# Sinkhorn of batch 0 in a chain of its own, the output projection of two batches by Strassen blocks, and an order of work given as a table

## The chip, the cores and the metric

The kernel runs on one core of a Trainium2 chip. The core has five engines that run side by side, each with its own queue of instructions that it takes in order: TensorE (PE, matrix products, into the eight PSUM banks), VectorE (DVE), ScalarE (ACT), GpSimd (POOL), and SyncE (SP), which here issues DMA transfers. TensorE loads the stationary operand of a matmul by a separate instruction (PEld). The metric is device time in microseconds (us), as a median over runs. Lower is better.

## The reference

Inputs q, k, v are of 4 batches, 8 heads, 768 positions, 64 features; `sort_net` gives an 8 by 8 matrix for each batch and head; the three weights of the second part are 512 by 1536, 512 by 1536 and 1536 by 512.

```
P = sort_net
for _ in range(5):
    P = exp(P - max(P, last axis))
    P = P / (sum(P, last axis) + 1e-9)        # rows
    P = P / (sum(P, second last axis) + 1e-9) # columns
k_sorted = einsum('bhij,bhjcd->bhicd', P, k_b)   # 8 blocks of 96 positions are mixed
v_sorted = the same with v
scores = q_b @ k_sorted_b.T / 8                  # within a block: 96 by 96
attn = softmax(scores);  x = attn @ v_sorted_b   # to 3072 tokens of 512
out = ((x @ w_a) * (x @ w_b)) @ w_out
```

## The kernel before

**A planner.** The kernel describes its work as pieces (`add`): an engine or a choice of engines with a duration for each, what a piece waits for, which buffers it gets and puts back, and a rank. `Plan.solve` walks through time greedily: of the pieces that could start first on each engine it takes the one of the lowest rank, at the engine that would end it first, and advances that engine's clock by the planned duration. The start times give the order in which the instructions are issued, so every engine's queue is in that order, and the planned durations (`LAT`, `EPS`, `AT` and the numbers at each `add`) matter only through it. `_fill` puts matmuls on a dummy tile (`warm_sb`) into the planned gaps of TensorE up to 32.6 us.

**Loads.** q, k, v and the weights come by DMAs that GpSimd issues and that turn fp32 into bf16 on the way, at most seven in flight (`load`). Batch 0 comes first, pair of heads by pair of heads, then column blocks 0 to 3 of `w_a` and `w_b` (`load_ab`, 384 columns each), the second halves of q of batch 0 in between, then batch 1, `w_out`, batch 2. GpSimd issues them in its one queue together with its elementwise work.

**Sinkhorn.** All 32 matrices lie in one tile `p_nat`, a partition for each batch and head (lines 412 to 425). A turn is an exp on ScalarE and six operations on VectorE: row sum, reciprocal, multiply, column sum, reciprocal, multiply. After five turns the result is widened (`p_rep`, half by VectorE, half by ScalarE) and brought across the partitions by eight small matmuls (`spread_ops`, line 435); `spread` (line 440) multiplies it with a mask into `s_all`, the matrix by which TensorE mixes blocks of k and v. The part of batch 0 is read from PSUM by VectorE; the others are spread later by GpSimd from a copy `p_col`.

**Attention.** For each pair of heads: transpose q, mix k and v by `s_all`, bring v to the layout that is needed, scores, exp, product with v, division by the row sum, and x transposed (`xT`). Batch 0 is done in halves of four blocks, so that the projections can start early; later batches send v, x, and in batch 3 also q, through DMA (V through DRAM, x and q by transposing DMAs), issued by SP.

**Projections.** Batch 0 uses plain products (`ab_plain`, line 749: for 12 column blocks and 2 halves of the tokens, four matmuls of 384 columns with `w_a`, four with `w_b`, then the gated product hT). Batches 1 to 3 use a Strassen scheme with seven products for eight (`ab_strassen`, line 831), which needs sums of weight blocks (`w_sums`, 16 operations, GpSimd alone) and of x blocks (`x_sums`), snapshots of PSUM by ScalarE (line 840) and additions by VectorE. All elementwise sums go through the helper `tt`, line 306.

**Output.** `out_plain` (line 899) does, for each batch, 2 halves of tokens by 3 chunks: twelve matmuls of 512 columns, a copy out of PSUM by ScalarE or VectorE (`copy`, lines 248 and 250), and two stores issued by SP (line 919). hT has one buffer, so gated products of the next batch wait for the output matmuls that read it (`out_last`).

The softmax here doesn't subtract the row's maximum and nothing guards it: scores larger than these inputs give would overflow.

## Time and profile before

| what | value |
|---|---|
| median of 3 runs | 245.04 us (244.59 to 245.09) |
| profiled execution | 245.06 us, of which the span of the core is 243.3 us |
| granted TensorE clock | 1.000 |
| busy: PE, DVE, ACT, POOL | 233.7, 150.1, 125.3, 119.6 us |
| matmuls | 2204 |
| DMA | 27.90 MB; the 16 engines are busy without a break from about 6 to 60 us |

In the lines below, a group reads: source line, engine, operation, tile written <- tiles read, shape, count. In a timeline the first two numbers are start and busy time; a bracket at the end gives the engine's idle time before and what released it. In a window row the pairs are busy time and instruction count of PE, PEld, DVE, ACT, POOL, then the granted clock, the DMA share and GB/s. A busy TensorE contains the dummy matmuls of `warm_sb`. Ends of matmuls are modelled.

### The profile page before, as it was taken

Reading aid. Unit: us, or ns where it says so; the run is one execution under the profiler, and the core shown is the slowest. Engines: PE = TensorE matmul, PEld = TensorE weight load, DVE = VectorE, ACT = ScalarE, POOL = GpSimd, SP = SyncE. Lnnn points to the kernel's source line nnn. Section 1 sums busy time; section 2 is a strip of 40 time slices with the busy share of each in tenths; the row PEclk is TensorE's granted clock in tenths of the full one; section 3 lists DMA queues with packets and bytes.
Section 4 is the critical chain, followed back from the end, with each engine's and each line's share of the span. In section 5 each row is a group of like instructions: output and inputs, shape, how many; then the busy total and the mean of one; then the engine's idle time right before and its main releaser. Section 6 shows DMA issues by size and latency. Waiting matters only on the chain.

```text
span 243.3 us, 5723 instructions
## 1 busy us (share of the span) xinstructions
PE 233.7 (96%) x2204; PEld 132.4 (54%) x2204; DVE 150.1 (62%) x348; ACT 125.3 (52%) x243; POOL 119.6 (49%) x132
## 2 busy tenths in 40 slices
PE   6998999999989999999999999999999999999992
PEld 2466766666655554665544455665654455565440
DVE  6656654654555738589987452988862448886210
ACT  3366646468655533667654443766631076673100
POOL 8979999999970020069755110173540007355000
PEclk9999999999999999999999999999999999999999
DMA  5999999999965683619998867200035450000135
GB/s 67 180 203 187 202 203 187 167 191 178 162 134 107 167 184 78 149 16 154 135 175 110 192 174 178 46 0 0 3 66 108 96 122 0 1 0 3 43 86 129
DMA packets 50106, 27.90 MB, mean 115 GB/s; under 512 B 28832, under 2 KB 47008, under 8 KB 50080
## 3 DMA queue, kind: packets, MB, share of 16 engines
q0 software_dynamic: 24112, 14.16, 43.3%
q1 hardware_dynamic: 25968, 13.38, 25.7%
q8 instruction: 17, 0.28, 0.5%
q14 instruction: 9, 0.07, 0.1%
HBM read 30.29 MB, written 8.26 MB: 158 GB/s over the span
## 4 chain that ended last, share of the span: by engine, by line
PE 67%; ACT 1%; DVE 1%; issue 0%; ACTq 0%; DVEq 0%
PE ps L831 33%; PE ps L899 26%; PE ps L593 2%; PE ps L578 2%; PE ps L489 1%; PE ps L537 1%; PE ps L473 1%; PE ps L749 1%; ACT f L840 0%; DVE xp L604 0%; ACT o L248 0%; DVE a L306 0%; DVE rec L599 0%; ACTq L840 0%; DVEq L306 0%
## 5 line engine op out<-in xcount | busy, mean ns | idle before, releaser
L306 POOL TENSOR_TENSOR hT<-a,f 128x384 bf16<-128x384 bf16 x39 | 35.5, 918 | 78.1 <-DVE f L306 56.3
L899 PE MATMUL ps<-w_out_sb,hT 128*128 128x512 bf16 x288 | 66.4, 379 | 0.0
L840 ACT COPY f<-ps 128x384 f32<-128x384 f32 x108 | 48.2, 482 | 23.6 <-PE ps L831 21.1
L899 PEld LDWEIGHTS <-hT 128*128 128x128 bf16 x288 | 27.0, 98 | 30.1
L306 DVE TENSOR_TENSOR a<-f,ps 128x384 bf16<-128x384 f32 x54 | 29.4, 549 | 10.4 <-PE ps L831 6.4
L306 DVE TENSOR_TENSOR f<-f,ps 128x384 f32<-128x384 f32 x54 | 28.9, 550 | 8.9 <-PE ps L831 6.0
L583 ACT ACTIVATE eT<-ps 96x768 bf16<-96x768 f32 x32 | 24.9, 806 | 17.2 <-PE ps L578 16.9
L306 DVE TENSOR_TENSOR hT<-a,ps 128x384 bf16<-128x384 bf16 x42 | 23.1, 551 | 12.4 <-PE ps L749 6.9
L248 ACT COPY o<-ps 128x512 f32<-128x512 f32 x15 | 8.8, 585 | 36.3 <-PE ps L899 36.3
L831 PE MATMUL ps<-tx,ws_a 128*128 128x384 bf16 x108 | 25.2, 326 | 0.2 <-ACT f L840 0.2
L831 PE MATMUL ps<-tx,ws_b 128*128 128x384 bf16 x108 | 24.9, 326 | 0.3 <-ACT f L840 0.3
L604 DVE TENSOR_TENSOR xp<-ps,rec 96x512 bf16<-96x512 f32 x32 | 21.4, 677 | 0.4
L749 PE MATMUL ps<-xT,w_a_sb 128*128 128x384 bf16 x96 | 19.6, 327 | 0.0
L749 PE MATMUL ps<-xT,w_b_sb 128*128 128x384 bf16 x96 | 19.6, 326 | 0.0
L831 PEld LDWEIGHTS <-ws_b 128*128 128x128 bf16 x144 | 13.8, 98 | 10.1 <-ACT f L840 0.9
L755 ACT CAST a<-ps 128x384 bf16<-128x384 f32 x24 | 11.5, 479 | 14.9 <-PE ps L749 9.1
L250 DVE COPY o<-ps 128x512 f32<-128x512 f32 x9 | 6.2, 691 | 20.8 <-PE ps L899 20.7
L831 PEld LDWEIGHTS <-ws_a 128*128 128x128 bf16 x144 | 13.5, 98 | 10.1 <-ACT f L840 1.4
L831 PE MATMUL ps<-xT,w_b_sb 128*128 128x384 bf16 x72 | 17.6, 326 | 0.3 <-DVE xp L604 0.2
L831 PE MATMUL ps<-xT,w_a_sb 128*128 128x384 bf16 x72 | 17.5, 326 | 0.0
L831 PEld LDWEIGHTS <-w_b_sb 128*128 128x128 bf16 x108 | 10.4, 98 | 7.9 <-DVE xp L604 0.7
L831 PEld LDWEIGHTS <-w_a_sb 128*128 128x128 bf16 x108 | 10.3, 98 | 7.9 <-ACT f L840 0.6
(90 smaller groups left out, 337.9 us busy)
## 6 DMA issues: line engine op xcount, KB each, us to landing
out_dram<-o SPq DMA_DIRECT2D x48, 128.0 KB, 2.4
k<-in_k_dram POOLq DMA_DIRECT2D x16, 192.0 KB, 6.1
v<-in_v_dram POOLq DMA_DIRECT2D x16, 192.0 KB, 6.1
vd<-vm SPq DMA_DIRECT2D x10, 192.0 KB, 2.9
vs<-vd SPq DMA_DIRECT2D x10, 192.0 KB, 3.1
q<-in_q_dram POOLq DMA_DIRECT2D x16, 96.0 KB, 6.9
w_a_sb<-in_moe_w_a_dram POOLq DMA_DIRECT2D x4, 384.0 KB, 7.1
w_b_sb<-in_moe_w_b_dram POOLq DMA_DIRECT2D x4, 384.0 KB, 9.0
```

What stands on the lines that cost most here:

```text
L248: nc.scalar.copy(out=out, in_=in_)
L250: eng.tensor_copy(out=out, in_=in_)
L306: ENG[eng].tensor_tensor(out=out, in0=in0, in1=in1, op=op)
L578: nc.tensor.matmul(sc[:, e, i * BLK:(i + 1) * BLK], lhsT=kT[e * D:(e + 1) * D, at:at + P], rhs=rhs, start=True, stop=True)
L583: nc.scalar.activation(out=buf(("eT", b, p, h))[:, :, 0:HB], in_=buf(("sc", b, p, h))[0:BLK, :, 0:HB], func=AF.Exp, scale=float(scale))
L593: nc.tensor.matmul(ops_[:, e, i * OW:(i + 1) * OW], lhsT=eT[:, e, i * BLK:i * BLK + P], rhs=vs[:, h * NBH + i, e * OW:(e + 1) * OW], start ...
L604: nc.vector.tensor_tensor(out=_ap(xp, h * NBH * 2 * D, [[NB * 2 * D, BLK], [D, 2], [2 * D, NBH], [1, D]]), in0=_ap(ops_, 2, [[1024, BLK], ...
L749: nc.tensor.matmul(pf[:, 0:HW], lhsT=w_sb[:, kc, m * P:(m + 1) * P], rhs=buf(("xT", b))[:, kc, t * HW:(t + 1) * HW], start=(kc == 0), stop ...
L755: ea = add("ACT", 0.48, lambda: nc.scalar.copy(out=buf(("a", b, t, m)), in_=buf(("pf", b, t, m, "a"))[:, 0:HW]), [pa], get=[("a", ("a", b, ...
L831: nc.tensor.matmul(buf(key)[:, 0:HW], lhsT=lf(j), rhs=rf(j), start=start and j == 0, stop=j == 1, skip_group_check=not start)
L840: return add("ACT", 0.48, lambda: nc.scalar.copy(out=buf((name, b, g, n)), in_=buf(kA)[:, 0:HW]), [dep], get=[("f", (name, b, g, n))], rank=r)
L899: nc.tensor.matmul(po, lhsT=hT[:, t * 2 + m // G, m % G, c * P:(c + 1) * P], rhs=w_out_sb[:, m, :], start=(m == 0), stop=(m == KO - 1), sk ...
```

## The change

**Sinkhorn.** The eight matrices of batch 0 get a chain of their own, with a partition for each head and row (64 partitions of 8 values, `pa`). In the first turn the row sum comes with the exp (`accum_out`), and a small fp32 matmul (`sk_turn`) turns the matrices so that the other sum lies along the free axis; in the four turns that follow the row sums over partitions are a small fp32 matmul with a mask of heads (`sk_rows`), and the remaining scale goes into the next exp as its `scale`. One matmul spreads the result (`spread_first`). Four small mask operations of VectorE are added. The 24 matrices of batches 1 to 3 keep the old chain, which now starts after batch 0's and has rank 12 instead of -9; its widening is one VectorE operation into a buffer of the ring `o`.

**Output.** Batches 2 and 3 use seven products for eight on blocks of hT and `w_out`: three chunks of seven products, each six matmuls of 256 columns. It needs eight sums of `w_out` blocks (`o_sums`), 24 sums of hT blocks for each batch, nine snapshots by ScalarE and twelve additions by VectorE for each batch. The stores of the last chunk are issued half by SP and half by ScalarE.

**Order.** A table `ORDER` of 1513 entries gives which piece comes next and on which of its engines; `solve` then only works out the planned times. The model changes as well: SP's DMAs get a clock of their own (`DH`), a `port` keeps planned GpSimd and VectorE sums apart, some durations and the load rate differ. `w_sums` may use VectorE for one of the two column blocks; the weight blocks are loaded in the order 0, 2, 1, 3; the ring `o` has four buffers instead of three; the first products of a Strassen batch wait for the `p5` of the last output chunk of the batch before (`lasty`) where that has one. `warm_sb` is now a part of `ws_b`.

```diff
-            pick = None
-            for e, c in cands.items():
-                lo = min(s for s, _ in c) + self.EPS[e]
-                s, op = min(((s, o) for s, o in c if s <= lo), key=lambda x: (x[1].rank, x[1].seq))
...
+        def given():
+
+            op = self.ops[order[done] // 2]
+            assert op in ready, "ORDER is not one of these pieces of work"
+            e = list(op.alts)[order[done] % 2]
+            return begin(op, e, max(self._when(op), op.ready)), e, op
...
+            s, e, op = given() if order else greedy()
...
-STRASSEN_OUT = ()
+RATE = 365e3
+ORDER = (
+    b"&,13###+#'#7#)#A#/#3#9#C#-#%$>#5#1#=$@$B#;$D#E#?$F$H#I$J#G$L#M$N#K$P#Q$R$T%l#O#U$V%n$X#Y$Z"
...
+STRASSEN_OUT = (2, 3)
...
-    for c in range(1, 4):
+    for c in (2, 1, 3):
         load_ab(c)
...
+    def sk_turn():
+        nc.tensor.matmul(buf(bank)[0:HN, 0:NB], lhsT=p_exp.rearrange("p h j -> p (h j)"),
+                         rhs=m_row, start=True, stop=True)
+
+    def sk_rows():
+        nc.tensor.matmul(buf(bank)[0:HN, NB:2 * NB], lhsT=m_same.rearrange("p h j -> p (h j)"),
+                         rhs=pa[:, 1, :], start=True, stop=True)
...
+    x = step("PE", 0.2, sk_turn, [x, o_row], get=[("bank", bank)])
+    x = step("DVE", 0.16, lambda: nc.vector.reduce_sum(
+        out=ps1, in_=buf(bank)[0:HN, 0:NB], axis=AX.X), [x])
+    x = step("DVE", 0.15, lambda: nc.vector.reciprocal(out=pc1, in_=ps1), [x], lat=0.1)
+    for it in range(4):
+        x = step("ACT", 0.3, lambda it=it: nc.scalar.activation(
+            out=pa[:, 1, :], in_=px if it else buf(bank)[0:HN, 0:NB], func=AF.Exp, scale=pc1), [x], lat=0.2)
+        x = step("PE", 0.12, sk_rows, [x, o_same])
+        x = step("DVE", 0.2, lambda: nc.vector.reciprocal(out=pr, in_=buf(bank)[0:HN, NB:2 * NB]),
+                 [x], put=[bank], lat=0.1)
+        x = step("DVE", 0.2, lambda: stt(px, pa[:, 1, :], 1.0, pr, ps1), [x], lat=0.02)
+        x = step("DVE", 0.15, lambda: nc.vector.reciprocal(out=pc1, in_=ps1), [x], lat=0.1)
...
         last = add("ACT", 0.26, lambda: nc.scalar.activation(out=p_nat, in_=p_nat, func=AF.Exp),
-                   [last], rank=-9)
+                   [last, o_p0], rank=12)
...
-            p1 = pe(kA, lambda j, w=w: w(0, 0, j), lambda j: xb(0, 0, j), True, False, x + wd, r,
+            p1 = pe(kA, lambda j, w=w: w(0, 0, j), lambda j: xb(0, 0, j), True, False,
+                    x + wd + [st.get(("lasty", b - 1))], r,
...
+            todo = ((0, lambda g=g: (hb(1, 0, g), hb(1, 1, g)), ALU.add, h21 + h22, None),
+                    (1, lambda g=g: (sb(0, g), hb(0, 0, g)), ALU.subtract, h11, 0),
+                    (2, lambda g=g: (hb(0, 0, g), hb(1, 0, g)), ALU.subtract, h11 + h21, None),
+                    (3, lambda g=g: (hb(0, 1, g), sb(1, g)), ALU.subtract, h12, 1))
...
+            p6 = pe(kA, s(1), wt(1), False, True, [s1] + sd(1) + td(1), rk, put=sput(1) + tput(1))
+            u2 = snap("ou2", p6)
+            p5 = pe(kY, s(0), wt(0), True, True, sd(0) + td(0), rk + 0.1, get=[("bank", kY)],
+                    put=sput(0) + tput(0))
+            st["lasty", b] = p5
+            p7 = pe(kA, s(2), wt(2), False, True, [u2] + sd(2) + td(2), rk, put=sput(2) + tput(2))
+            u3 = snap("ou3", p7)
+            p4 = pe(kZ, h(1, 1), wt(3), True, True, [p1, p2] + hd(1, 1) + td(3), rk + 0.6,
+                    get=[("bank", kZ)], put=tput(3))
+            c22 = plus("ou3", kY, 1, 1, [u3, p5], [("ou3", b, c)])
+            c21 = plus("ou3", kZ, 1, 0, [u3, p4], [kZ, ("ou3", b, c), ("och", b, c)])
+            p3 = pe(kY, s(3), wo(1, 1), False, True, [c22] + sd(3), rk, put=sput(3))
+            c12 = plus("ou2", kY, 0, 1, [u2, p3], [kY, ("ou2", b, c), ("och", b, c)])
...
+                    (nc.scalar if last and u else nc.sync).dma_start(
```

## The prediction

> **What bounds the kernel now.** I read the page first, for the engines' shares and the chain of work that ended last; then the waits of TensorE; then the timeline, at the start, around the two last output stages and at the end; then the windows, to see what the other engines have free there.
>
> The page:
>
> ```profile
> span 243.3 us, 5723 instructions
> PE 233.7 (96%) x2204; PEld 132.4 (54%) x2204; DVE 150.1 (62%) x348; ACT 125.3 (52%) x243; POOL 119.6 (49%) x132
> ...
> PE 67%; ACT 1%; DVE 1%; issue 0%; ACTq 0%; DVEq 0%
> ```
>
> TensorE is busy in 96% of the span, and the chain, which begins only at 72 us, is TensorE but for 1% each of ScalarE and VectorE. "Busy" needs a second look, because the kernel also issues matmuls on a dummy tile, `warm_sb`. The timeline of the start:
>
> ```profile
> 2.29 0.26 ACT L414 ACTIVATE p_nat<-p_nat 32x64 f32<-32x64 f32 x1 [0.27 <-DMA p_nat<-in_sort_net_dram]
> ...
> 4.05 0.26 ACT L414 ACTIVATE p_nat<-p_nat 32x64 f32<-32x64 f32 x1 [1.50 <-DVE p_nat L424]
> ...
> 10.84 0.21 DVE L424 TENSOR_TENSOR p_fin<-p_nat,csum 32x64 bf16<-32x64 f32 x1
> 11.99 0.61 ACT L248 COPY p_rep<-p_fin 32x512 bf16<-32x512 bf16 x1
> 13.47 0.36 PE L435 MATMUL ps<-ident,p_rep 32*128 32x32 bf16 x8
> 13.95 1.29 DVE L440 TENSOR_TENSOR s_all<-mask,ps 128x256 bf16<-128x256 bf16 x2 [2.45 <-PE ps L435]
> 14.42 0.38 PE L500 MATMUL ps<-s_all,k 128*64 128x64 bf16 x12
> 27.46 0.82 PE L749 MATMUL ps<-xT,w_a_sb 128*128 128x384 bf16 x4
> ```
>
> Until 14.42 TensorE does four groups of q transposes (0.38 each) and otherwise dummies: the Sinkhorn chain (turns of 1.76 us, 2.29 to 4.05) is the path. From 27.46 the long projections run, four matmuls in 0.65, and TensorE is full to the last matmul at 238.68. Between them it does about 10.8 us of batch 0's attention in 13.0. After 27.46 the gaps that the timeline and chain show are 0.8 at 71.2, 0.6 at 118.4, 0.6 at 126.0, 1.2 at 151.0 and 1.1 at 210.8: 4.2 us together. So time comes off the end in three ways: an earlier end of the Sinkhorn, less TensorE work, a shorter tail.
>
> Windows around the output stages of batches 2 and 3 (busy of PE, PEld, DVE, ACT, POOL in each), and three groups behind the elementwise helper:
>
> ```profile
> 160.00:180.00 20.00, 20.00 (x125) 11.96 (x123) 16.79 (x34) 13.16 (x31) 10.58 (x12) 1.00 0.11 21
> 180.00:200.00 20.00, 20.00 (x102) 9.74 (x101) 7.33 (x14) 5.66 (x13) 1.18 (x2) 1.00 0.46 99
> ```
>
> ```profile
> L306 POOL TENSOR_TENSOR hT<-a,f x39: 910/918/925, 104.3 to 223.4; 128x384 bf16<-128x384 bf16 x39
> L306 DVE TENSOR_TENSOR tx<-xT x5: 547/550/554, 81.1 to 188.9; 128x768 bf16<-128x768 bf16 x5
> L306 POOL TENSOR_TENSOR tx<-xT,tx x1: 1831/1831/1831, 139.1 to 139.1; 128x768 bf16<-128x768 bf16 x1
> ```
>
> While a batch's gated product runs, VectorE is 84% busy; while the output projection runs it is 37% busy and GpSimd nearly idle.
>
> **The change, part by part.** The profiled execution took 245.06, 1.76 beyond its span of 243.3, and stands 0.02 above the median of 245.04; the sum is made against it.
>
> *Sinkhorn of batch 0.* A turn was exp 0.26, six VectorE operations of 0.19 to 0.25, and gaps of 0.03 to 0.04. The new turn is exp, a tiny fp32 matmul, reciprocal 0.19, multiply 0.21, reciprocal 0.19, four hand-offs of 0.03 to 0.04: 0.99 plus the matmul x. No row shows a lone fp32 matmul. Below, x is an eighth of the 0.36 group at 13.47 plus its hand-off of 0.12 to VectorE: 0.17; above, the whole group, 0.48. I take 0.40, nearer to the upper, since fp32 is unlikely to cost what bf16 does. First turn 1.63, four turns of 1.39, final multiply, matmul and hand-offs 0.50: 7.7 from 2.29, so the spread starts at 10.0. With every x low it is 8.8; with every x high and 0.2 in each turn for the accumulated sums, which no row shows, 11.6. VectorE also gets four small mask operations at the start, and the ScalarE and TensorE queues between the turns hold q copies and dummies, so I take 10.6: 3.4 earlier than 13.95 (ends 2.3 and 5.2). The p_rep copy of ScalarE and its wait (11.05 to 13.47) leave with it.
>
> Is anything late next? The last v of batch 0 is issued at 8.93 and lands 6.6 later, at 15.5, and was read at 20.92; the first weights of w_b land at 20.3 (10.89 plus 9.4) and were read at 28.12. These have 5 and 8 us to spare. But the weight loads now come in the order 0, 2, 1, 3: block 1 lands where block 2 did, w_b at 30.6, and its first reader at 32.58 moves to about 29. What hides this is the other work there (3.4 us of batch 0's second halves, and block 2's projections); without it, it costs 1.4.
>
> The Sinkhorn of batches 1 to 3, 35 operations, now comes after: on VectorE 5 times 1.26 plus a widening and a copy, about 7.5 us, on ScalarE 1.3. From 12 to 45 VectorE is idle for 13 us, and GpSimd's spreads (2.0 each), which wait for it and have the load issues behind them in their queue, are not needed before batch 1's mix at 48.37. Spread evenly it costs nothing; falling wholly before 27 it would delay the evacuations there by up to half, 3.7. I take 0.7. Front: 3.4 less 0.7, a gain of 2.7 (ends 0.5 and 4.0).
>
> *Output of batches 2 and 3 by Strassen blocks.* Out: 72 matmuls of 512 columns a batch at 0.2158 (2.59 for twelve), 15.5 us. In: three chunks of seven products of six matmuls of 256 columns, 126. That width is not in the trace. The 384 wide take 0.1626 (0.65 for four), the 128 wide transposes 0.056 with a weight load each (0.45 for eight), so weight loads are no floor, and the line between them gives 0.109: 13.7 us. Gain 1.8 a batch, 3.6 (ends 2.9 at twice the 128 wide pitch, 3.9 at half the 512's).
>
> The cover: per batch 24 sums of hT blocks; the order table gives 11 of batch 3's to GpSimd (0.92, the hT row), 13 to VectorE (two bf16 inputs; 0.35 from 0.55 for twice the width): 10.1 and 4.6 us. Nine snapshots by ScalarE (0.37, from 0.48 at 384) and twelve additions by VectorE (0.41) replace six copies of 0.59 to 0.69. Eight w_out sums come once. In 160 to 180 VectorE has 3.2 free, so some of its sums fall after the gated product, whose last hT write ends 3.7 us after the first output matmul (182.80 plus 0.56, against 179.69). TensorE has p1, p2 and p4 of three chunks, nine groups of 0.65, 5.9 us, which need no sums. That just covers 3.7, two chained sums and a short queue. In batch 2 the new dependence `lasty` holds every gated product of batch 3 behind the last chunk's p5; TensorE is in order, so a wait there stops everything. I take 0.4 a batch, 0.8 (ends 0 and 3 a batch).
>
> A row on the shared port: GpSimd's tx sum at 139.1 took 1.83 against 1.63 at 89.6; VectorE was in a sum of two bf16 tiles for its first 0.34. So GpSimd stands still for about 0.6 of such an overlap, while its hT products, beside VectorE operations with a PSUM input, keep to 910 to 925 ns. Thirteen sums of 0.35 take at most 2.7 us from it a batch, on 10 us in a stage where it has 9.4 free: inside the bound of 3. The Trainium skill (GPSIMD Engine Reference, Specifications) says that GpSimd and VectorE share SBUF interfaces and contend when VectorE reads two SBUF inputs. It speaks against this change: read as a full stop over all 13 VectorE sums, an estimate from it is 4.6 a batch where the row gives 2.7; were all of either turned into waits of TensorE in place of my 0.4, the time would be 246.3 by the page and 242.5 by the row.
>
> *Tail.* The last copy (0.59), two store issues on one queue to 240.42 and 2.87 to the end make 4.61 after 238.68. Now an addition of 0.41 and one issue of 0.57 on each of SP and ScalarE: 3.9. Gain 0.7. In the table p7 of the last chunk is followed by a sixth of p2, p5, p4, then p3: 1.41 of work against 1.33 for the addition that p3 waits for. No stall.
>
> *The order.* Of the 4.2 us of gaps a new order may close some and open others; I take a gain of 1.0 (ends a gain of 2.5, a loss of 2.0).
>
> Sum: 2.7 + 3.6 + 0.7 + 1.0 - 0.8 = 7.2; 245.06 - 7.2 = 237.9.
>
> **Rivals.** *The front hardly gains.* The later Sinkhorn and batch 0's evacuations share VectorE and ScalarE (11.9 and 12.0 of 18 us busy in 12 to 30); front 0.5, order nothing, waits 1.6: 0.5 + 3.6 + 0.7 - 1.6 = 3.2, 241.9. For it: both engines are as loaded as TensorE there. Against: the operations are small, and have until 45.
>
> *All of it comes.* Front 4.0, output 3.9, tail 0.7, order 2.5, no waits: 11.1, 234.0. For it: 5 us of slack on the last load. Against: the order must be right to tenths in five queues.
>
> *Slower: the sums come late.* In the stage before the output VectorE (21.07 of 25.2 busy from 154.5 to 179.7) has no room for 4.6 more, and GpSimd needs 12.16 + 10.1 + 2.7 of 25.2. If the last sums are later than the cover by d, TensorE stops for d in each batch. Without my 0.8 the gain is 8.0, so it decides from d = 4.0; at 6 the time is 249. Against: after 180 both engines are nearly free, and 24 sums on two engines are some 5 us even if none was done early.
>
> *No effect*: the parts cancel within 0.2% (0.5 us), about what a measurement of this kernel can tell from no change; no mechanism of its own.
>
> **How the numbers follow.** The sum, 236 to 240.2: 0.55. All of it, 233 to 236: 0.15. The front hardly gains, 240.2 to 244: 0.18. No effect 0.02, slower 0.10. Faster 0.55 + 0.15 + 0.18 = 0.88. The range 234.2 to 242.6 leaves out 0.05 below and 0.15 above.
>
> **What would show it.** Right: the first mix matmul near 11 instead of 14.4; the first long projection near 24.5; the two output stages at 0.65 for six matmuls; the last matmul near 232 with under 4 us behind it. Wrong: dummies or idle time before the output products that read the sums; VectorE or ScalarE without a gap from 11 to 27; a lone fp32 turn of 1.8 or more; matmuls of batch 0 at half their rate, as the first eleven dummies now are (0.42 for 512 columns, later 0.22), because TensorE pauses in every turn.

## The result, and the profile after

The changed kernel took 261.09 us (median; 260.23 to 262.45) against 245.03 us for the kernel before: a ratio of 1.0665, interval 1.0617 to 1.0713. It is 16 us slower where 7 us of gain were forecast. The profiled execution took 260.97 with a span of 259.2.

The page of the changed kernel, the lines that answer to those shown of before:

```profile
span 259.2 us, 6049 instructions
...
PE 236.4 (91%) x2306; PEld 144.5 (56%) x2306; DVE 178.2 (69%) x418; ACT 127.6 (49%) x257; POOL 150.0 (58%) x164
...
PEclk9999799999999999599999999999999599999999
...
PE 79%; DVE 8%; DMA 6%; issue 2%; POOL 2%; ACT 0%; DVEq 0%; ACTq 0%
```

TensorE is busy 2.7 us longer, though it has less to do, and stands 22.8 us in place of 9.6. VectorE has 28 us more and GpSimd 30 us more; both now stand in the chain, with DMA. The clock row has three notches that were not there before, in slices 5, 17 and 32 of 6.5 us each.

The waits of TensorE (engine, tile and line, what it waited for; total, times, longest):

```profile
PE ps L1145 <- DVE v L391: 5.9, 1, 5.9
PE ps L742 <- DMA vs<-vd: 4.7, 2, 4.3
PE ps L649 <- issue: 2.9, 2, 1.7
PE ps L899 <- ACT a L905: 1.3, 1, 1.3
```

Where the time went can be read from the start and end of the stages, all from the timelines of TensorE and VectorE (the last column is a version of experiment 3):

| us | before | after | later by | all three edits undone (3) |
|---|---|---|---|---|
| first spread of s_all | 13.95 | 12.28 | -1.7 | - |
| first long projection | 27.5 | 28.4 | +0.9 | 27.8 |
| output of batch 0, first matmul | 75.9 | 79.7 | +3.8 | 79.3 |
| output of batch 1, first matmul | 129.4 | 140.3 | +10.9 | 133.2 |
| output of batch 2, last matmul | 195.9 | 213.0 | +17.1 | 200.1 |
| last matmul ends | 238.7 | 254.2 | +15.5 | 241.3 |
| end of the span | 243.3 | 259.2 | +15.9 | 245.7 |

So there are three places of loss: 3.8 before the output of batch 0, 7 in that stage, 6 before the end of batch 2's output. Only behind the last one does the changed kernel gain: from the last output matmul of batch 2 to the last matmul of all it needs 41.2 us where the kernel before needs 42.8.

**The third place.** The timeline where batch 2's sums of hT blocks are made; the tiles `k` and `v` hold the sums, `tx` the x sums of batch 3:

```profile
194.75 1.10 DVE L391 TENSOR_TENSOR k<-hT 128x384 bf16<-128x384 bf16 x1
...
197.74 0.35 DVE L391 TENSOR_TENSOR v<-v,hT 128x384 bf16<-128x384 bf16 x1
198.81 3.45 POOL L391 TENSOR_TENSOR tx<-xT 128x768 bf16<-128x768 bf16 x2
...
200.69 1.78 DVE L391 TENSOR_TENSOR v<-hT 128x384 bf16<-128x384 bf16 x1
202.53 0.82 PE L1145 MATMUL ps<-q,k 128*128 128x256 bf16 x3 [5.88 <-DVE v L391]
...
206.99 0.50 PE L1145 MATMUL ps<-q,v 128*128 128x256 bf16 x3
```

A VectorE sum of this shape takes 0.35 when GpSimd rests (197.74), 1.06 to 1.10 beside GpSimd's sums of the same shape, and 1.78, twice, beside the twice as wide ones (198.81: two of them). TensorE stands 5.88 for them. Then three matmuls of 256 columns take 0.82 (0.64 from start to start) until about 206.3, where they later take 0.50 (0.33): the clock is down, which costs another 1.9.

**The second place.** The chain of work in order of time:

```profile
96.18 10.80 DMA vs<-vd
...
107.62 4.09 PE ps L1052 x10
```

TensorE waits for batch 2's V, which comes back from DRAM 10.8 us after its issue. The ten output matmuls behind it take 0.41 each in place of 0.22. The median trip of these transfers is 5.1 us here and 3.1 before. Nothing in this stage is a part of the change as I had read it; GpSimd issues the first ten of batch 3's loads at 92.2 to 100.3 here (the rest from 125 on), where the kernel before issues them all at 107.2 to 119.5, behind the last of these transfers.

In the windows of 100 to 120 and 200 to 220 us the granted clock is 0.83, in the others from 30 us to 240 it is 1.00: these are two of the notches. The third lies in the first place.

**The first place.** VectorE among GpSimd's weight sums, and TensorE in the middle of batch 0's mixing:

```profile
25.09 0.25 PE L649 MATMUL ps<-s_all,k 128*64 128x64 bf16 x4 [1.73 <-issue]
41.20 1.65 POOL L391 TENSOR_TENSOR ws_b<-w_b_sb 128x768 bf16<-128x768 bf16 x1
41.96 2.56 DVE L567 TENSOR_TENSOR p_nat<-p_nat,csum 24x64 f32<-24x64 f32 x1
...
50.94 2.19 DVE L323 COPY o<-p_fin 24x1024 bf16<-24x1024 bf16 x1
```

The multiply of 2.56, across this weight sum and the next, takes 0.21 elsewhere; the copy of 2.19, which runs beside another weight sum (50.86), takes 0.67 where GpSimd rests.

The third notch is here too. The first 30 us, before:

```profile
0.00:30.00 30.00, 26.63 (x447) 16.30 (x448) 20.27 (x90) 15.93 (x32) 27.22 (x37) 1.00 1.13 167
```

and after, with the first group of long projections (before, such a group took 0.82):

```profile
0.00:30.00 30.00, 24.57 (x425) 15.22 (x426) 17.33 (x91) 14.77 (x32) 23.57 (x36) 0.94 1.14 169
...
28.40 1.34 PE L899 MATMUL ps<-xT,w_b_sb 128*128 128x384 bf16 x4
```

From about 26.1 to 29.5 TensorE runs at half rate, behind stops of only 1.2 (at 18.75) and 1.7 (at 25.09). 3.4 us at half rate cost up to 1.7, about 1.2 of it before 28.4 (an estimate from these times).

**Theories.** First: VectorE, working from SBUF alone, waits while GpSimd adds two SBUF tiles; this carries the third place, and perhaps a part of the first. Second: batch 3's loads, ahead of their planned place, delay V; this carries the second place. Rivals: the table of order is bad as a whole; the 24 sums are too much for the stage on any engine; the Sinkhorn chain of batches 1 to 3 is late in itself.

### The profile page after: what moved, and what is told of

Same layout as the page of the kernel before. It is cut to its first block, busy times and chain, and to the rows that moved or that the text cites. A ratio compares the mean times of both kernels' runs of the same rounds, so it can differ in the third digit from the quotient of the medians.

```text
span 259.2 us, 6049 instructions
## 1 busy us (share of the span) xinstructions
PE 236.4 (91%) x2306; PEld 144.5 (56%) x2306; DVE 178.2 (69%) x418; ACT 127.6 (49%) x257; POOL 150.0 (58%) x164
## 3 DMA queue, kind: packets, MB, share of 16 engines
q1 hardware_dynamic: 25876, 13.12, 23.8%
## 4 chain that ended last, share of the span: by engine, by line
PE 79%; DVE 8%; DMA 6%; issue 2%; POOL 2%; ACT 0%; DVEq 0%; ACTq 0%
PE ps L982 31%; PE ps L1052 12%; PE ps L1145 11%; PE ps L899 9%; DMA vs<-vd 4%; PE ps L742 3%; PE ps L727 3%; DMA q<-in_q_dram 2%; PE ps L638 2%; PE ps L649 2%; DVE v L391 2%; PE ps L622 2%; PE ps L686 1%; PE ps L708 1%; DVE p_nat L567 1%
## 5 line engine op out<-in xcount | busy, mean ns | idle before, releaser
L391 POOL TENSOR_TENSOR hT<-a,f 128x384 bf16<-128x384 bf16 x46 | 41.9, 924 | 37.8 <-DVE f L391 29.6
L991 ACT COPY f<-ps 128x384 f32<-128x384 f32 x108 | 48.9, 482 | 29.9 <-PE ps L982 27.6
L1052 PE MATMUL ps<-w_out_sb,hT 128*128 128x512 bf16 x144 | 36.4, 396 | 0.0
L732 ACT ACTIVATE eT<-ps 96x768 bf16<-96x768 f32 x32 | 25.5, 807 | 17.2 <-PE ps L727 17.0
L1052 PEld LDWEIGHTS <-hT 128*128 128x128 bf16 x144 | 13.2, 101 | 14.8 <-issue 2.2
L899 PE MATMUL ps<-xT,w_a_sb 128*128 128x384 bf16 x96 | 18.8, 327 | 1.6 <-ACT a L905 1.3
L748 DVE RECIPROCAL rec<-ps 96x8 f32<-96x8 f32 x32 | 6.2, 199 | 20.1 <-PE ps L742 18.7
L899 PE MATMUL ps<-xT,w_b_sb 128*128 128x384 bf16 x96 | 19.0, 333 | 0.0
L1166 ACT COPY f<-ps 128x256 f32<-128x256 f32 x18 | 6.7, 372 | 23.1 <-PE ps L1145 23.1
L321 ACT CAST kT<-ps 128x768 bf16<-128x768 f32 (+1 forms) x18 | 12.4, 692 | 11.2 <-PE ps L638 6.9
L742 PE MATMUL ps<-vs,eT 96*128 96x66 bf16 x256 | 13.4, 195 | 4.7 <-DMA vs<-vd 4.7
L982 PE MATMUL ps<-xT,w_a_sb 128*128 128x384 bf16 x72 | 17.4, 326 | 0.0
```

The costliest lines, as they stand in the source:

```text
L321: nc.scalar.copy(out=out, in_=in_)
L391: ENG[eng].tensor_tensor(out=out, in0=in0, in1=in1, op=op)
L732: nc.scalar.activation(out=buf(("eT", b, p, h))[:, :, 0:HB], in_=buf(("sc", b, p, h))[0:BLK, :, 0:HB], func=AF.Exp, scale=float(scale))
L742: nc.tensor.matmul(ops_[:, e, i * OW:(i + 1) * OW], lhsT=eT[:, e, i * BLK:i * BLK + P], rhs=vs[:, h * NBH + i, e * OW:(e + 1) * OW], start ...
L899: nc.tensor.matmul(pf[:, 0:HW], lhsT=w_sb[:, kc, m * P:(m + 1) * P], rhs=buf(("xT", b))[:, kc, t * HW:(t + 1) * HW], start=(kc == 0), stop ...
L982: nc.tensor.matmul(buf(key)[:, 0:HW], lhsT=lf(j), rhs=rf(j), start=start and j == 0, stop=j == 1, skip_group_check=not start)
```

## The experiments

**1. The order, and the output part.** The changed kernel without the table, so that the old greedy search orders the work by the new model; and the same with plain output for all batches.

```diff
-ORDER = ( ... )
+ORDER = b""
-STRASSEN_OUT = (2, 3)
+STRASSEN_OUT = ()          # second version only
```

> The changed kernel without its table: the order comes from the greedy walk again, with all the new work and the new model. Theory 3 (the table has no slack, and with slack the new work pays): 245 or less. Theory 1: the sums still run on both engines, and the small Sinkhorn still beside GpSimd's weight sums, so most of the loss stays: 252 to 262.

> As the greedy one, but with the plain output for all batches: the new Sinkhorn, the new model and the freer weight sums alone. Theory 1: no sums of hT blocks, so the stop of 5.9 us before the output of batch 2 is gone, but the Sinkhorn of batches 1 to 3 still lies beside GpSimd's weight sums: 244 to 250. If the Sinkhorn part is sound by itself, 1.7 us as the first spread is earlier: 243.4. If the loss is all in the front: 253 or more.

Measured 257.0 and 249.5, one run each. The table itself costs about 4, but without it most of the loss stays. With plain output and no table, so with the Sinkhorn, the model, the new order of weight loads and the freer weight sums, 4.5 of the loss are still there: it lies in more than one part.

**2. VectorE beside GpSimd, by itself.** A program that leaves the whole computation out: groups of six equal VectorE operations, alone and beside six GpSimd sums of two SBUF tiles.

> A kernel of its own that leaves the whole computation out and writes zeros: six operations at a time on VectorE, on GpSimd, or on both. Theory 1 (shared port): an operation that reads two SBUF tensors on VectorE and one on GpSimd exclude each other, and the later one waits for the end of the earlier. Then the 384 wide bf16 sum, 0.35 us alone on VectorE, has a mean of 0.8 to 1.3 beside GpSimd sums of 0.92; the fp32 multiply of 24 x 64, 0.21 alone, lasts up to 1.65 beside GpSimd's 768 wide sums; the sum with a PSUM operand keeps 0.55 and the reduction 0.21. Rival (the long VectorE operations of the changed kernel came from DMA traffic or from their queue): each keeps its time alone within 0.05 in every phase. For the sums beside issues of GpSimd loads theory 1 says nothing; the 1.37 us sum at 49.0 in the changed kernel would mean that the issue holds the port too.

Its timeline: sums alone and beside GpSimd, sums with an operand in PSUM beside GpSimd, small multiplies alone and beside GpSimd:

```profile
7.28 1.67 DVE L54 TENSOR_TENSOR yd<-xd,zd 128x384 bf16<-128x384 bf16 x6
...
14.84 5.26 DVE L54 TENSOR_TENSOR yd<-xd,zd 128x384 bf16<-128x384 bf16 x6 [5.89 <-ACT xd L94]
...
21.47 2.87 DVE L59 TENSOR_TENSOR yf<-fd,ps 128x384 f32<-128x384 f32 x6 [1.36 <-ACT ps L94]
...
27.49 0.89 DVE L64 TENSOR_TENSOR yf<-fd,gd 24x64 f32<-24x64 f32 x6 [3.15 <-ACT fd L94]
...
28.88 8.14 DVE L64 TENSOR_TENSOR yf<-fd,gd 24x64 f32<-24x64 f32 x6 [0.50 <-ACT fd L94]
```

A VectorE sum goes from 0.28 to 0.88, the tiny multiply from 0.15 to 1.36, a copy of 128x1024 from 0.35 to 1.55 (2.10 and 9.29 for six): whatever its own length, it waits for about one GpSimd instruction. GpSimd loses little (5.23 to 5.82 for six). Sums with an operand in PSUM (2.87, 0.48 each) and reductions (0.84 for six of 24x64 beside GpSimd, 0.14 each) are not held. The DMA issues of the last group fell elsewhere in time, so this program says nothing about them. The Trainium skill (Trainium Architecture — The Big Picture, What this means for kernel authors) calls the ports that the two engines share an exclusive lock and not a split of bandwidth; these numbers agree.

Two more such programs asked whether GpSimd's DMA issues hold VectorE too, since one multiply of experiment 5 took 4.95 us across two sums and two issues.

> A probe that leaves the whole computation out (zeros are stored). Six VectorE operations, alone and then beside six GpSimd DMA issues that start with them: sums of 128x384 bf16, fp32 multiplies of 24x64, copies of 128x1024 bf16. Theory 1 (a GpSimd DMA issue holds VectorE as a GpSimd sum does, which would explain a multiply of 4.95 us at 29.73 to 34.68 in the version with the new Sinkhorn alone, across two sums and two issues of GpSimd): each group takes 4 us or more beside the issues of about 0.73 each. Theory 2 (issues leave VectorE alone): within 0.3 of the groups alone, 1.7, 0.9 and 2.1.

> A probe that leaves the whole computation out (zeros are stored). Twelve fp32 multiplies of 24x64 of VectorE alone (1.6 to 1.8 in all) and beside three rounds of a GpSimd sum of 128x768 (1.63) and a DMA issue (0.73) behind it; then twelve copies of 128x1024 bf16 alone (4.2) and beside three issues, each behind a tiny copy. Theory 1 (sums hold VectorE, issues do not): several multiplies end inside each issue, all twelve within two rounds, some 5 us; the copies stay at 4.2 to 4.7. Theory 2 (issues hold it as well): a multiply ends only once in a sum or issue, twelve take over 7 us, the copies 6 or more.

In the first only one issue fell into a group, which took 1.70 in place of 1.68: not held. In the second, twelve multiplies (1.63 alone) took 7.11, beside two sums from 8.77 and then this:

```profile
8.84 7.11 DVE L62 TENSOR_TENSOR yf<-fd,gd 24x64 f32<-24x64 f32 x12
11.94 1.58 POOL L51 DMA_DIRECT2D ld<-in_q_dram  x2
13.54 1.65 POOL L54 TENSOR_TENSOR ld<-xp,zp 128x768 bf16<-128x768 bf16 x1
```

Of its single records, two multiplies end behind the first two sums (10.47, 12.07), four end inside the first issue (12.20 to 12.61), and one lasts from 12.54 to 15.27, through the second issue and the sum behind it, so that it was held 1.0 before that sum began; the last three end inside an issue with no sum behind it. The twelve copies beside three issues took 4.26 against 4.12. So in these groups an issue alone does not hold VectorE, and neither theory of the expectation is met as a whole: the copies fit the first, the 7.11 in total fits the second. That GpSimd takes the port as soon as a sum is next in its queue would fit the multiply held 1.0 and the 4.95; it was seen once in each and not tested further. And the changed kernel has one sum of two SBUF tiles that is slow beside nothing but issues, where the same shape takes 0.55 elsewhere:

```profile
48.01 2.18 POOL L461 DMA_DIRECT2D k<-in_k_dram  x3
49.04 1.37 DVE L391 TENSOR_TENSOR ws_b<-w_b_sb 128x768 bf16<-128x768 bf16 x1
```

No program here explains it, so whether an issue alone can hold VectorE stays open.

**3. The three places, one at a time and together.** The changed kernel with its table. Batch 3's first load waits for batch 2's last x (a tiny copy on GpSimd reads it); the sums of hT, w_out and x blocks run on VectorE alone, x of all three Strassen batches; the weight sums run on VectorE alone.

```diff
+        if (b, p) == (3, 0):
+            nc.gpsimd.tensor_copy(out=hold, in_=buf(("xp", 2, 3))[:, NB - 1, 1, 0:2])
...
-                op = add((("DVE", 0.33), ("POOL", 0.92)), None, None,
+                op = add((("DVE", 0.33),), None, None,
...
-            al = (("POOL", 1.75), ("DVE", 0.55)) if c == 1 else (("POOL", 1.75),)
+            al = (("DVE", 0.55),)
```

> The changed kernel with its table, and one tiny GpSimd copy ahead of the loads of batch 3 that reads the last attention result of batch 2, so that those loads really wait for it. Theory 2 (the loads of batch 3 run ahead of their place in the plan and crowd the DRAM round trip of batch 2's V): the waits of TensorE for vs (4.7 us) and the wait chain of 10.8 us at 96 shrink to under 3 us, and the time falls by 5 to 9, to 252 to 256. Theory 1 alone: the V trip is late because VectorE was, and the time stays within 2 of 261.

> The changed kernel with its table of order, and one edit: the sums of w_out blocks, of hT blocks and of batch 3's x blocks run on VectorE alone, at the same places of the order. Theory 1 (VectorE and GpSimd exclude one another in sums of two SBUF tiles, and only VectorE's sums are slowed threefold by it): the sums before the output of batch 2 take 0.35 each in place of 1.06 to 1.78, TensorE's stop of 5.9 us before the first matmul that reads S is gone and the slow clock in 200 to 220 too; 8 to 9 us shorter than the change, 252 to 254, with the loss around 96 to 112 still there. Theory 2 (the 24 sums are simply too much work for that place, whatever engine does them): VectorE alone needs 24 x 0.35 = 8.4 us where two engines shared them, so the stop stays or grows; 260 to 263.

> The changed kernel with its table of order, and one edit: the sixteen sums of weight blocks run on VectorE alone. Theory 1 (VectorE's Sinkhorn products and its widening copy wait for GpSimd's two-tile sums in 41 to 55 us): the multiply of 2.56 and the copy of 2.19 fall to about 0.2 and 0.5, the first output matmul of batch 0 comes 2 to 3.5 us earlier than at 79.8, and the whole is 257 to 259.5. Theory 2 (the batches 1 to 3 Sinkhorn is late for another reason, its own length or its place in the order): the first output matmul of batch 0 stays within 0.7 of 79.8, or is later by VectorE's added 16 x 0.55 us; 260.5 to 264.

> The changed kernel with its table, batch 3's loads held back and the sums of hT, x and w_out blocks on VectorE alone; the weight sums stay where the table has them. Against the version with the weight sums on VectorE too (247.6): if the collisions at 41 to 55 us cost the 3.8 that the first output matmul of batch 0 came late, this is 250 to 252; if they are made up for elsewhere, 247 to 248.5, and if moving the weight sums cost more than it brought (that version has a stop of 2.1 behind VectorE's V copy), 245 to 247.

> The changed kernel with its table of order and three edits together: all sums of two SBUF tiles on VectorE alone, and batch 3's loads held back until batch 2's x and V have been through their transfers. If the three places of loss (41 to 55, 96 to 112, 194 to 203 us) are apart from one another and have the causes named, their gains add: 2 to 3.5 plus 5.5 plus 8, so 244 to 246, and the granted clock is above 0.98. If a fourth cause carries a good part of the loss (the order itself, VectorE overfull with some 10 us more of sums), it stays above 249.

| edits | us |
|---|---|
| none | 261.09 |
| loads held back | 255.62 |
| sums on VectorE | 258.23 |
| weight sums on VectorE | 262.79 |
| loads and sums | 248.03 |
| all three | 247.62 |

Each row but the first is one run. Four runs of the changed kernel lie between 260.2 and 262.5, and versions with the same front start the output of batch 0 at 79.7 (none), 80.5 (sums), 81.0 (loads) and 79.5 (both), so a difference below some 2 us between two rows tells nothing.

The loads are worth 5.5. Their stop fell from 4.3 to 0.6, and the clock in 100 to 120 is 1.00 again.

The sums are worth 7.6 once the loads are held back: 5.88 of stop and 1.9 of slow clock are 7.8. Without that, 2.9: the stop in the output of batch 0 grew (TensorE waits 5.1 for VectorE at 90.5 to 95.6, which has an x sum in front that waits for its transfer, 8.1 us), and in that run the clock of the first 30 us was 0.85 in place of 0.94. VectorE alone does the 24 sums in time: the stop before the first product that reads them is 0.3, as the waits of the version with all three show.

```profile
PE ps L711 <- DVE vT L323: 2.1, 1, 2.1
...
PE ps L1148 <- DVE v L392: 0.3, 1, 0.3
```

So the rival "too much work" falls.

The weight sums missed. The collisions are gone (no multiply of the chain above 0.21, the copy 0.67), and yet the output of batch 0 starts no earlier: at 81.0, and with all three edits at 79.3 against 79.5 with two. The 0.4 between 248.03 and 247.62 can't be told from nothing: a wait of 1.3 (L899, for ScalarE's `a`) goes, and the wait for vT, behind a weight sum on VectorE, grows from 0.5 to 2.1. So this edit takes work from one engine and gives it to another that is in the way; what it shows is that the first place is not explained by those two slow instructions alone. Of the expectations, the sums alone (252 to 254) and all three (244 to 246) missed, and loads and sums fell in the middle of three (247 to 248.5: made up for elsewhere).

**4. The output part alone.** The kernel before with its Sinkhorn, model and greedy order, plus the Strassen output with hT and w_out sums on VectorE: for batches 2 and 3; the same with batch 3's x sums off GpSimd as well; for batch 3 alone; and that with half of batch 3's stores in its first two chunks issued by GpSimd.

```diff
-STRASSEN_OUT = ()
+STRASSEN_OUT = (2, 3)      # third and fourth version: (3,)
...
-        al = (("DVE", 0.55), ("POOL", 1.75))
+        al = (("DVE", 0.55),) if b == 3 else (("DVE", 0.55), ("POOL", 1.75))   # second version
...
-                    (nc.scalar if last and u else nc.sync).dma_start(
+                    (nc.scalar if last and u else nc.gpsimd if u else nc.sync).dma_start(   # fourth
```

> The kernel before, with its Sinkhorn, its greedy planner and its models as they were, and one part of the change: output of batches 2 and 3 by Strassen blocks, with the sums of hT and w_out blocks on VectorE alone. Theory 1 (the output part is worth the 1.7 us a batch that batch 3's stage showed, once its sums do not run against GpSimd's): 241 to 242.5. Theory 2 (24 more VectorE operations in a stage where VectorE is 84 per cent busy are late whatever runs beside them): TensorE stops before the first matmul that reads S by 3 us or more in each batch; 247 to 252.

> As the kernel before with Strassen output of batches 2 and 3 and the sums of hT and w_out blocks on VectorE alone, and one more edit: batch 3's sums of x blocks, which GpSimd ran at 185 to 192.5 beside them, are on VectorE alone as well. Theory 1 (what made the 24 sums late was VectorE taking turns with GpSimd's x sums: 0.88 to 1.1 each in place of 0.3): TensorE's stops of 3.0 and 5.5 before batch 2's products fall to under 1.5 together, 241.5 to 246. Theory 2 (the place is too full for 24 sums, and eight of w_out, whatever runs beside them): VectorE's total rises by six sums of 0.55 more, so the stops stay at 8 or grow; 253 to 257.

> The kernel before with Strassen output of batch 3 alone, sums of hT and w_out blocks on VectorE alone: no x sums of a later batch can meet them. If a batch's output stage is worth 1.6 to 1.8 and the tail nothing: 242.8 to 244.2. If the 24 sums are late even here: TensorE stops before the first product that reads S, and the time is 245 or more.

> The version with Strassen output of batch 3 alone (245.4; last matmul 2.0 earlier than before, but 6.7 us from it to the end in place of 4.6, with SP issuing twelve stores one after another from 233.4 to 240.5), with half of the stores of batch 3's first two chunks issued by GpSimd, idle there. If SP's queue is what gives the gain back: last matmul still at 236.5 to 237, the tail 4.0 to 4.6, 242.6 to 243.6, a ratio of 0.990 to 0.995 to the kernel before. If the stores' transfers themselves are the limit: within 0.3 of 245.4.

| version | us | ratio to before (interval) | TensorE, output of batch 2 to last matmul | last matmul to end |
|---|---|---|---|---|
| before | 245.03 | 1 | 42.8 | 4.6 |
| batches 2, 3 | 254.46 | 1.0406 (1.0327 to 1.0484) | 41.1 | 5.8 |
| and x sums off GpSimd | 246.96 | 1.0081 (1.0052 to 1.0110) | 41.4 | 6.5 |
| batch 3 alone | 245.39 | 1.0003 (0.9979 to 1.0027) | 41.2 | 6.7 |
| and stores split | 245.05 | 0.9980 (0.9960 to 0.9999) | 41.2 | 6.2 |

The ratios are to runs of the kernel before taken beside each version (medians 245.2 to 245.5), so a time and its ratio need not agree to the last digit. The first version is slower than either of its theories had.

The first version has two stops, 3.0 and 5.5, and the third place again. None of the new sums is on GpSimd here, but those of batch 3's x blocks are (185.4 to 192.5). A timeline:

```profile
187.52 3.49 DVE L306 TENSOR_TENSOR k<-hT 128x384 bf16<-128x384 bf16 x2
...
193.98 0.88 DVE L306 TENSOR_TENSOR v<-v,hT 128x384 bf16<-128x384 bf16 x3
```

Two VectorE sums take 3.49 beside them, three take 0.88 afterwards. With six sums more on VectorE, the version is 7.5 faster: only the first theory has that direction, though its size was missed: what stays are stops of 1.5 and 1.5, so batch 2 gains nothing.

In all versions TensorE needs 1.4 to 1.7 less for batch 3. But the tail takes it back. In the version with batch 3 alone the last matmul ends at 236.7, 2.0 earlier than before, and the last VectorE addition at 237.2; then SP is still issuing:

```profile
236.53 2.74 SPq L1056 DMA_DIRECT2D out_dram<-s_all  x4
240.01 0.54 SPq L1056 DMA_DIRECT2D out_dram<-s_all  x1
```

In the greedy order the last products of the three chunks come together at the end, so eight stores at 0.54 to 0.78 stand in SP's queue from 235.3 to 240.6, where the plain output has two stores in 2.6 us. Half of them on GpSimd's queue brought 0.5 of the tail back, nearer to the second theory than to the first: SP's last two issues then took 1.18 and 1.08. This version is the only one that the interval puts below the kernel before, by 0.2%, no more than a measurement can tell. A version whose chunks end one after the other was not measured.

A last program, without the computation, timed the stores themselves.

> A probe that leaves the whole computation out (zeros are stored). Six fp32 multiplies of 24x64 with a broadcast operand alone (0.9 in all) and beside three GpSimd sums of 128x768 with a DMA issue behind each. If VectorE only waits for the sum that runs (turns): six multiplies end within about 3 sums, 5 to 7 us. If the issues hold it too: no multiply ends inside an issue, and single ones take over 2.3 us. Then twelve stores of 128 KB on SP, six of 256 KB on SP, twelve of 128 KB on SP and ScalarE by turns, twelve on SP and GpSimd. Theory 1 (SP's issue is the limit, and per store): 12 take 7.2 to 9 us to issue, the six of 256 KB half of it, two queues half of it. Theory 2 (the bytes are the limit, or two queues share what issues): all four groups take about the same, and issues of SP beside another queue's take 0.8 to 1.2 in place of 0.6.

Of twelve stores of 128 KB on SP ten took 0.55 to 0.60 each to issue, one 0.47, and the first, behind the larger stores, 4.91; while ScalarE issues too they took 0.54 to 0.86. The six of 256 KB (pairs of rows in one transfer) moved 51 GB/s, and each issue from the third on took 3.4 to 7.2. The groups ran into one another, so this is no clean comparison, but it speaks against fewer, larger stores of this pattern; the kernel was not measured with them. Beside four store issues of GpSimd six VectorE sums of 128x768 took 2.90, 0.48 each: not held.

**5. The Sinkhorn part alone.** The kernel before with the new Sinkhorn, nothing else; the same with the 24-matrix chain at rank -6 in place of 12; and with the spreads of batches 1 to 3 on VectorE.

```diff
-                   [last, o_p0], rank=12)
+                   [last, o_p0], rank=-6)      # second version, the whole chain
...
-            o = add("POOL", 2.0, lambda b=b: spread(nc.gpsimd, p_col, BL, b * H - H, H, b * H),
+            o = add("DVE", 1.38, lambda b=b: spread(nc.vector, p_col, BL, b * H - H, H, b * H),   # third
```

> The kernel before with one part of the change: the Sinkhorn of batch 0 apart with row sums on TensorE, the 24 other matrices after it at rank 12; planner, models, order of loads, plain output as before. Theory A (the earlier s_all reaches the long projections): first spread at 12.3 in place of 13.95, first long projection about 1.7 earlier, 243.0 to 244. Theory B (something else starts the projections: loads, instruction stops of TensorE, ScalarE's and VectorE's queues): the projections start within 0.6 of 27.5, 244.5 to 246. Theory C (the moved 24-matrix chain meets GpSimd's two-tile weight sums on VectorE, as in 41 to 55 us of the change): p_nat multiplies of over 1 us are seen and the output of batch 0 starts 2 us or more late, 247 to 249.5.

> The version with the new Sinkhorn alone (253.3), with the 24-matrix chain at rank -6, ahead of batch 0's attention work and so ahead of GpSimd's weight sums from 28 us on, in place of rank 12. Theory 1 (the loss comes from the chain lying among GpSimd's two-tile sums): no multiply of the chain above 0.5 us, GpSimd does not stand before the spreads, first output matmul of batch 0 within 1.5 of the 75.9 before, 244 to 247. Theory 2 (the loss comes from VectorE and ScalarE having 35 and 5 operations more among batch 0's evacuations, wherever they lie): the projections start later still, 29 or more, and the time stays at 249 to 254.

> The version with the new Sinkhorn alone (253.3), with the spreads of batches 1 to 3 on VectorE in place of GpSimd, so that no load stands behind them in GpSimd's queue. If the loads that stood 7 us behind the first spread carry the loss: 246 to 249, and TensorE's wait of 2.4 for V at 78 us is gone. If VectorE's waits for GpSimd carry it: the multiply of about 5 us and TensorE's wait for x at 35 are still there, and it stays at 250 to 254.

The first took 253.32 (ratio 1.0305, 1.0247 to 1.0364): the part that was forecast as the second largest gain costs 8 us by itself, more than any theory had. The spread starts 1.3 earlier (12.62), the first long projection 1.9 later (29.4), the output of batch 0 8.2 later (84.1). Its first 30 us and its timeline:

```profile
0.00:30.00 30.00, 26.45 (x455) 16.77 (x459) 17.71 (x94) 15.89 (x34) 22.14 (x35) 0.94 1.13 168
...
29.73 4.95 DVE L493 TENSOR_TENSOR p_nat<-p_nat,csum 24x64 f32<-24x64 f32 x1
...
46.38 1.99 POOL L513 TENSOR_TENSOR s_all<-mask,p_col 128x1024 bf16<-128x1024 bf16 x1 [6.99 <-ACT p_col L248]
...
78.44 0.60 PE L668 MATMUL ps<-vs,eT 96*128 96x66 bf16 x8 [2.44 <-DMA vs<-vd]
```

A tiny multiply stands in VectorE's queue for 4.95 beside GpSimd's weight sums and issues, and the evacuations of batch 0 behind it: TensorE waits 2.44 for x at 35.4. The chain ends late, so GpSimd stands 7 us before the first spread, with the last load of batch 1, `w_out` and batch 2 behind it in its queue; at 78 TensorE waits for a V.

The slow clock at the front is here as well, and comes from this part: TensorE runs at half rate from 20.4 to 23.8, behind one stop of 1.6. In the window of 20 to 30 us the granted clock is 0.54 to 0.90 in every profiled version that has the new Sinkhorn, and 1.00 in the kernel before and in the four versions of experiment 4, which have the old one. Why the new front brings it stays open.

The early chain took 251.89 (1.0253, 1.0207 to 1.0300): a miss for its theory 1; the time is in the range of theory 2, whose later projections did not come (28.6). Its multiplies take at most 0.96, but its operations lie one by one between the evacuations in VectorE's queue and end at 36.0, and GpSimd still stands 5.6 before the spread. The third took 259.76, the other way than expected: three spreads on VectorE took 9.30 from 49.37 beside GpSimd's weight sums, and TensorE then stood 4.3.

What of the 8 is VectorE's wait, what GpSimd's empty wait and what the slow clock is not settled; taking the first away brought the second. Nor is the 8 a fixed price: with the model, load order and weight sums of the changed kernel (experiment 1, plain output) the same Sinkhorn leaves a loss of 4.5.

## Why the prediction was wrong

**The rows on the shared port, read for the wrong engine.** "So GpSimd stands still for about 0.6 of such an overlap" took the one overlapping row (GpSimd's 1.83 against 1.63) as the price and gave it to GpSimd. It is mostly VectorE that stands, for about one GpSimd instruction: 0.35 becomes 1.06 to 1.78. The rows could not show it: VectorE's own tx sums were all 547 to 554 ns, and the one that met a GpSimd sum (139.1) was running first. The term "I take 0.4 a batch, 0.8 (ends 0 and 3 a batch)" was therefore far too small, and its bound of 3 was no bound: batch 2 lost 5.9 of stop and 1.9 of slow clock, 7.8, of which 7.6 came back when the sums left GpSimd. The estimate from the page, 246.3, had the right sign and named the right contention; its price was too low as well, since it counted VectorE's own 13 sums of 0.35, and the wait goes by the length of GpSimd's instruction.

**The rival "the sums come late" came true in batch 2.** Its point of decision was a stop of 4.0 in each batch, 8.0 in all; measured are 7.8 in batch 2 with the slow clock and none in batch 3, where no x sums of a next batch run on GpSimd. So this alone takes the forecast gain back, and does not make the kernel slower by 16. Its reason was wrong: VectorE has room for all 24 sums.

**The Sinkhorn of batches 1 to 3: "Spread evenly it costs nothing", "I take 0.7".** I counted idle time of VectorE from 12 to 45, not whose turn it was: the multiplies and the copy among those 35 operations work from SBUF and lie among weight sums; and every one waits in order behind evacuations. That GpSimd's spreads "are not needed before batch 1's mix" was true of the spreads and not of the loads behind them, which I had named. The part alone costs 8 where 2.7 was to be gained, so the term "a gain of 2.7" failed with the 0.7 in it; how the 8 divides is open.

**The turn.** Turns took 1.5 to 1.7 where I had 1.39: reciprocal starts 0.42 to 0.64 after the exp ends, for which I had 0.40, with 0.48 as upper end; the accumulator is read by an instruction of its own, 0.07 on VectorE and 0.19 on ScalarE. The first exp came at 2.70 in place of 2.29, and the spreading matmul stood 0.8 behind q transposes. So 12.28 and not 10.6. Of the 1.7 that were left nothing reached the projections: TensorE's stops in mid-group were 2.9 in place of 1.0, and the half rate before 28.4 took about 1.2 (the estimate above). The prediction's own sign, matmuls of batch 0 at half their rate, did come, but at 26 to 29.5, long after the turns, and not by the pause in every turn that it gave as the reason.

**The order: "a gain of 1.0 (ends a gain of 2.5, a loss of 2.0)".** The "4.2 us of gaps" were pieces of other engines in the chain: TensorE itself stood only 0.78, 0.25, 0.29, 0.17 and 0.10 at those five places, 1.6 in all, so there was little for a new order to close. And I looked at gaps and not at what keeps the order. Batch 3's loads have only a planned time; once TensorE was late, GpSimd ran ahead with them, and V came late. Holding them back gave 5.5; that it was the share of the DMA engines that V lacked is read from the traces.

**Right:** the 256-wide matmul, 0.109 taken, 0.113 measured (115 in 13.00); the output stage, 1.8 taken, 1.4 to 1.7 measured for batch 3. Batch 2 gained nothing in the versions looked at. **The tail** was 5.0 and not 3.9: ScalarE's store issue took 1.33 once, and the store landed 2.7 to 3.4 after its issue.

The sum in runs: loads 5.5, sums 7.6, remaining 3.0 above before (248.03 against 245.03), which is 3.6 late at the output of batch 0 (79.5 against 75.9), less what batch 3 gains. In that version TensorE's idle time up to 80 us is 7.6 against 4.2 before (30, 30 and 20 us less the busy 24.5, 28.1 and 19.9; before 26.6, 30.0 and 19.2); the waits that can be named are mid-group stops of 1.9 (1.0 before), q by 1.8 (1.1) and ScalarE's `a` by 1.3 (none). Beside this idle time stands the slow clock of the first 30 us, 0.94 in that version too, some 1.8 us of work by an estimate (0.06 of 30). That division is read from the traces, not tested.

## What to carry to other kernels

Before a sum moves to VectorE or GpSimd, list what the other does at that moment: two engines with free time each may have none together. A plan's time is not a wait: what only a planned time holds back will run ahead as soon as something else is late. Measure each part of a composite change alone; here the part that looked safest, the earlier Sinkhorn, cost 8 us alone, and the part that works, the output of the last batch, was paid back in the store queue.

## What the runs showed of the hardware

- VectorE operations that read and write SBUF alone (sums, multiplies, copies) wait for GpSimd's sums of two SBUF tiles, about one for one: 0.28 to 0.88, 0.15 to 1.36, 0.35 to 1.55. Those with an operand in PSUM (0.48 each) and the reductions tried (0.14 each) do not wait. Beside DMA issues of GpSimd alone, sums and copies were not held (1.70 against 1.68, 4.26 against 4.12), but one sum of the changed kernel took 1.37 in place of 0.55 there: open.
- After stops of 4.3 and 5.9 TensorE ran at half rate for about 4 us (0.41 for 512 columns against 0.22). The Trainium skill (TensorE: Matmul & The Clock Gate, Part 1: The HAM clock gate (the "warmup" mystery)) has a half clock after an idle window of some 3.4 us and as long to come back; these two stops agree. That rule does not cover the half rate from 26.1 to 29.5, which came behind stops of 1.2 and 1.7; a slow clock at the front goes with the new Sinkhorn in every profiled version here and is not explained.
- TensorE's stops in mid-group in the first 26 us, with nothing to wait for, each end 1.2 to 1.5 after a transfer of 16 KB on the instruction queue has landed (18.43 and the stop's end 19.86 before; 17.52 and 18.75, 23.67 and 25.09 after). One more such transfer of before (landed at 23.2) has no stop behind it. The three fit a wait for its own instructions; no run tested it.
